# Moving one batch's attention from the hidden layer into the projection, and rearranging the conversion of float64 weights

## The chip, the cores and the metric

The kernel runs on one core of a Trainium2 chip. The metric is the device time of one execution in microseconds (us); the time of a kernel is the median of its runs.

## What is computed

The inputs are `x` (8 batches, 8 heads, 512 tokens, 64 features), `state` (8 batches, 8 heads, 32 states, 64 features), and the weights of a gated layer, which reach the kernel as float64. In the reference, cut to what matters:

```python
scores = scale * (x @ state.T);  a = softmax(scores);   xread = a @ state
scores2 = scale * (state @ x.T); a2 = softmax(scores2); sread = a2 @ x
y = concatenate([xread, sread], axis=2)          # (8, 8, 544, 64)
t = y.transpose(0, 2, 1, 3).reshape(8 * 544, 512)
tn = t / sqrt(mean(t * t) + 1e-6) * rms_g
out = (silu(tn @ w_gate) * (tn @ w_val)) @ w_out  # 512 -> 1536 -> 512
```

## The kernel before, in words

**Order of the work.** The program goes over the 8 batches. For each it computes attention, the hidden layer (1536 units in 12 blocks `m` of 128) and the projection to 512 columns; the states of all batches come at the end, as 256 rows together. `attention(b)` (L211) is a generator of 17 steps, and its steps are put between other work by `some(n)`, which takes the next n of them. Before the first hidden layer, attention of batch 0 runs alone up to its tokens, then values and the first four weight pieces, then the rest of attention of batch 0. In batch 0 the hidden layer is a loop over `m`; after every `m` it takes three steps of attention of batch 1, so that all 17 lie in the first six rounds. Batches 1 to 7 use another form, with seven products for eight blocks (`hidden_seven`, `project_seven`), and take steps of attention of the next batch in both. A scheduler lays the instructions of each engine out in a fixed order, by the order in the program and by when it reckons operands to be there; on the chip each engine then takes its instructions strictly in that order, and a waiting instruction holds those behind it.

**Weights.** A weight piece is 1 MB of float64: 128 partitions times 1024 pairs of 32-bit words. There are 18: twelve for gate and value (two for each pair of blocks `m`) and six for the output. `load_piece` (L134) loads up to four ahead, into four buffers, on SP's queue. `to_float32` (L163) turns a piece into float32, with eight operations: the exponent field is cut from the high words (L183, VectorE), clamped and moved into place by two Relu (L185, L186, ScalarE); the low words are scaled (L188, ScalarE Copy); the high mantissa gets its leading one (L189), is scaled and added to the low part (L190); the sign is put to the exponent (L192); and mantissa times exponent gives the weight (L196). L189 to L196 are VectorE's. `ready(n)` (L152) converts pieces up to n. Converted pieces of gate and value are also written back to a scratch in DRAM (L161), from which the later batches fetch them (L127); they share three buffers.

**Values and hidden layer.** `make_v` (L375) multiplies converted weights by the states (L381, PSUM pool `vps`) and copies the result out (L388). `hidden` (L401) multiplies it by the attention weights of the tokens (L407), and tanh (L412, ScalarE) and two VectorE operations (L413, L415) give the hidden block `hb`. In batch 0 the value product for a pair of blocks waits for two converted pieces.

**Projection of batch 0.** `project_as_ready` (L484) accumulates four PSUM banks over 12 blocks (L493), in the pools `fx`, `fy` and `fz`; before every second `m` it calls for one more converted piece of the output weights and then `between(m)`. At `m = 8` this converts all that is left, opens the buffers of the later batches in the space of the raw ones, and prepares batch 1: `slot_sums` (L428, four operations on GpSimd, POOL) and the first `make_v` of batch 1. Batch 1 begins with L445.

**Attention.** Transposes of x (L232) are copied out by ScalarE (L233); scores (L240, L249) are transposed (L259), reduced, shifted and exponentiated (L263 to L266), normalised (L273 to L276), transposed back (L281, L284) and multiplied by the states (L291). Only the mean of squares of this read is needed here: four Square on ScalarE (L297) give `sq`, two VectorE adds bring four blocks to one (L300, L301), four one-column matmuls sum over the partitions (L304), L307 adds the small constant, a power on POOL gives the inverse root (L206), which is spread by L209 and multiplied into the attention weights (L310). Then follow the states' reads (L316 to L347). At its start attention of batch b issues the loads of state and x of batch b + 1 (L83, L88). Its PSUM tiles come from `aps`, and two of the four reads from `vps`, which `make_v` uses too.

Of the kernel before, what the change touches and what calls it, by code (L numbers as in the profile page):

```python
# [8 lines left out]
F32 = mybir.dt.float32  # L9
I32 = mybir.dt.int32  # L10
U32 = mybir.dt.uint32
ALU = mybir.AluOpType
ACTF = mybir.ActivationFunctionType
AXX = mybir.AxisListType.X
# [2 lines left out]
P = 128  # L17
# [5 lines left out]
def kernel(  # L23
# [20 lines left out]
    VE, SE, GE, TE = nc.vector, nc.scalar, nc.gpsimd, nc.tensor  # L44
# [15 lines left out]
    two = ctx.enter_context(tc.tile_pool(name="two", bufs=2))  # L60
# [35 lines left out]
    ones = consts.tile([P, 1], F32, name="ones")  # L96
    GE.memset(ones, 1.0)
    bounds = consts.tile([P, 2], F32, name="bounds")
    GE.memset(bounds[:, 0:1], 1151.0)
    GE.memset(bounds[:, 1:2], 255.0 * (1 << 23))  # L100
    rms_g = consts.tile([P, NI], F32, name="rms_g")

# [26 lines left out]
    def home(k):  # L129
        if k >= NM:  # L130
            m = 2 * (k - NM)
            return wo[:, m:m + 2].rearrange("p m (i f) -> p m i f", f=P)
        mp = k // 2
        return (w_sb[mp] if k % 2 else new_w(mp))[:, :, :, k % 2, :]  # L134

    def load_piece(k):
        if k >= len(pieces):
            return
        src = pieces[k]
        if src.dtype == F32:  # L140
            return
        raw[k] = raws.tile([P, 8 * P, 2], I32, name="raw")
        out_ = raw[k].rearrange("p (a f) two -> p a (f two)", a=src.shape[1])
        for a in parts(k):
            nc.sync.dma_start(out=out_[:, a], in_=src[:, a].bitcast(I32))

    def parts(k):

        n = pieces[k].shape[1]
        return (slice(0, n // 2), slice(n // 2, n)) if k == 0 else (slice(0, n),)  # L150
# [13 lines left out]
    def to_float32(k):  # L164


        load_piece(k + RAW_AHEAD)
        to = home(k)
        if k not in raw:
            src = pieces[k].rearrange("p a (c f) -> p a c f", f=P)  # L170
            for a in range(src.shape[1]):
                nc.sync.dma_start(out=to[:, a], in_=src[:, a])
            return
        whole = raw.pop(k)
        tops = conv.tile([P, 8 * P], I32, name="top")
        exs = conv.tile([P, 8 * P], I32, name="ex")
        n = pieces[k].shape[1]
        for a in parts(k):
            cols = slice(8 * P * a.start // n, 8 * P * a.stop // n)
            r, top, ex, dst = whole[:, cols, :], tops[:, cols], exs[:, cols], to[:, a]  # L180
            hi = r[:, :, 1]
            man = r.bitcast(F32)[:, :, 0]
            VE.tensor_scalar(ex, hi, 20, 0x7ff, op0=ALU.logical_shift_right, op1=ALU.bitwise_and)  # L183

            SE.activation(out=ex, in_=ex, func=ACTF.Relu, scale=-1.0, bias=bounds[:, 0:1])  # L185
            SE.activation(out=ex, in_=ex, func=ACTF.Relu, scale=-float(1 << 23),  # L186
                          bias=bounds[:, 1:2])
            SE.activation(out=man, in_=r.bitcast(U32)[:, :, 0], func=ACTF.Copy, scale=2.0 ** -52)  # L188
            VE.tensor_scalar(top, hi, 0xfffff, 0x100000, op0=ALU.bitwise_and, op1=ALU.bitwise_or)  # L189
            VE.scalar_tensor_tensor(out=man, in0=top, scalar=2.0 ** -20, in1=man,  # L190
                                    op0=ALU.mult, op1=ALU.add)
            VE.scalar_tensor_tensor(out=ex, in0=hi, scalar=-(1 << 31), in1=ex,  # L192
                                    op0=ALU.bitwise_and, op1=ALU.bitwise_or)
            man, ex = (t.rearrange("p (a c f) -> p a c f", f=P, c=dst.shape[2])
                       for t in (man, ex.bitcast(F32)))
            VE.tensor_tensor(out=dst, in0=man, in1=ex, op=ALU.mult)  # L196


    stT_g = {}
# [3 lines left out]
    def inverse_rms(ss, n):  # L203

        ri = two.tile([P, NC], F32, name="ri")
        GE.tensor_tensor(out=ri[:, 0:n], in0=ss, in1=mhalf[:, 0:n], op=ALU.pow)  # L206
        rp = aps.tile([P, NC, P], F32, name="at")
# [4 lines left out]
    def attention(b):  # L212
        xb, packed = x_sb.pop(b), rows.pop(b)
        if b + 1 < B:
# [7 lines left out]
                     in_=packed.rearrange("p e d -> p (e d)"), identity=ident)  # L222
        VE.tensor_copy(stT, tp)
        VE.tensor_tensor(out=stT_g[b], in0=stT, in1=rms_g.unsqueeze(2).to_broadcast([P, 4, Ns]),
                         op=ALU.mult)
# [11 lines left out]
        sp = [aps.tile([P, S], F32, name="at") for e in range(2)]  # L237
        for j in range(4):
            for e in range(2):
                TE.matmul(out=sp[e][Ns * j:Ns * j + Ns, :], lhsT=stT[D * e:D * e + D, j, :],  # L240
                          rhs=xT[j // 2][D * e:D * e + D, j % 2].rearrange("p c t -> p (c t)"),
                          start=True, stop=True)
# [12 lines left out]
        for cp in range(2):  # L255
            tp = aps.tile([P, 2, 2, P], F32, name="at")
            for c in range(2):
                for e in range(2):
# [6 lines left out]
                             op=ALU.subtract)  # L265
# [4 lines left out]
        for cp in range(2):  # L270
# [6 lines left out]
                             op=ALU.mult)  # L277
            tp = aps.tile([P, 2, 2, P], F32, name="at")
            for c in range(2):
                for e in range(2):  # L280
                    TE.transpose(out=tp[:, c, e, :],  # L281
                                 in_=eS[:, 2 * cp + c, e].rearrange("p j n -> p (j n)"),
# [6 lines left out]
        for j in range(4):  # L289
            for e in range(2):  # L290
                TE.matmul(out=reads[j][D * e:D * e + D, :],  # L291
                          lhsT=packed[Ns * j:Ns * j + Ns, e, :],
                          rhs=aT[Ns * j:Ns * j + Ns, e].rearrange("n c t -> n (c t)"),
                          start=True, stop=True)
        sq = [one.tile([P, 2, S], F32, name="sq%d" % i, tag=("xT1", "eS")[i]) for i in range(2)]
        for j in (2, 3, 0, 1):
            SE.activation(out=sq[j // 2][:, j % 2, :], in_=reads[j], func=ACTF.Square,  # L297
                          scale=DM ** -0.5)
        yield
        VE.tensor_tensor(out=sq[1], in0=sq[1], in1=sq[0], op=ALU.add)  # L300
        VE.tensor_tensor(out=sq[0][:, 0, :], in0=sq[1][:, 0, :], in1=sq[1][:, 1, :], op=ALU.add)  # L301
        sp = aps.tile([P, NC], F32, name="at")
        for c in range(NC):
            TE.matmul(out=sp[:, c:c + 1], lhsT=sq[0][:, 0, P * c:P * c + P], rhs=ones,  # L304
                      start=True, stop=True)
        ss = two.tile([P, NC], F32, name="ss")
        VE.tensor_scalar(ss, sp, 1e-6, None, op0=ALU.add)  # L307
        yield
# [2 lines left out]
                         in1=rp.unsqueeze(1).to_broadcast([P, 2, S]), op=ALU.mult)  # L311
# [7 lines left out]
        for e in range(2):  # L319
            SE.activation(out=e2[:, e], in_=sS[:, e], func=ACTF.Exp, scale=SCALE,  # L320
                          bias=s2[:, e:e + 1], accum_out=z2[:, e:e + 1])
# [11 lines left out]
        for e in range(2):  # L333
            for c in range(NC):
                for j in range(4):
                    h = 2 * j + e
                    TE.matmul(out=rp[Ns * j:Ns * j + Ns, e, :],
                              lhsT=e2T[:, e, c, Ns * j:Ns * j + Ns],
                              rhs=xb[:, c, D * h:D * h + D],
                              start=(c == 0), stop=(c == NC - 1))  # L340
        sr = two.tile([P, 2 * D], F32, name="sr")
        for e in range(2):
            VE.tensor_scalar(sr[:, D * e:D * e + D], rp[:, e, :], z2[:, e:e + 1], None,
                             op0=ALU.mult)
# [5 lines left out]
    def state_norm():  # L350

        sq = one.tile([P, NI, NT], F32, name="sqT", tag="eS")
        SE.activation(out=sq, in_=xsT, func=ACTF.Square, scale=DM ** -0.5)
        sp = aps.tile([P, NT // P], F32, name="at")
        for r in range(NT // P):
            for i in range(NI):
                TE.matmul(out=sp[:, r:r + 1], lhsT=sq[:, i, P * r:P * r + P], rhs=ones,
                          start=(i == 0), stop=(i == NI - 1))
        ss = two.tile([P, NT // P], F32, name="sst")
        VE.tensor_scalar(ss, sp, 1e-6, None, op0=ALU.add)  # L360
        rp = inverse_rms(ss, NT // P)
        for i in range(NI):
            VE.scalar_tensor_tensor(out=xsT[:, i, :], in0=xsT[:, i, :], scalar=rms_g[:, i:i + 1],
                                    in1=rp[:, 0:NT], op0=ALU.mult, op1=ALU.mult)
        yield
# [257 lines left out]
    def some(n):  # L623
        for _ in range(n):
            next(steps, done)

    for b in range(B):
        if b > 0:
            steps = attention(b + 1) if b + 1 < B else state_norm()
        else:  # L630
            for m in range(NM):
                if m % 2 == 0 and m + 2 < NM:
                    make_v(b, m // 2 + 1)
                v, _ = v_sb[b, m // 2]
                hidden(m, S, lambda e, k: v[:, e, m % 2, k, :],
                       [aT_s[b][:, e, :] for e in range(2)])
                some(3)

            def between(m):
                if m == NM - 4:  # L640
                    ready(len(pieces))
                    early.close()
                    open_late()
                    prepare(b + 1)

            project_as_ready(store_tokens(b), between)
            sums = weight_sums()
        if b > 0:
            pairs = [hidden_seven(b, mp) for mp in range(NM // 2)]
            next(pairs[0])  # L650
            for mp, pair in enumerate(pairs):
                if mp + 1 < len(pairs):
                    make_v(b, mp + 1)
                next(pair)
                if mp + 1 < len(pairs):
                    next(pairs[mp + 1])
                next(pair)
                some(2)
                next(sums, done)
            project_seven(S, store_tokens(b), lambda: some(5), lambda: prepare(b + 1))  # L660
        for _ in steps:
            pass
        for _ in sums:
            pass
# [36 lines left out]
```

## Time and profile before

| what | value |
|---|---|
| median of three runs | 877.27 us (876.86 to 879.85) |
| the profiled execution's own time | 877.27 us |
| its span, first to last instruction | 875.5 us |
| PE (TensorE matmul) busy | 829.3 us, 95% |
| DVE (VectorE) busy | 473.2 us, 54% |
| ACT (ScalarE) busy | 341.6 us, 39% |
| POOL (GpSimd) busy | 156.2 us, 18% |
| TensorE's mean granted clock | 0.970 |
| first record of the hidden layer of batch 0 (L407) | 48.25 us |
| last conversion operation (L196) ends | 141.2 us |
| first record of batch 1's hidden layer (L445) | 161.68 us |

Times within the profile are counted from the first instruction. TensorE's matmuls overlap and their ends are modelled, so that a busy TensorE isn't one at its peak; a float32 matmul shows as two records, a transpose as one. Starts of successive records tell the pace better than the durations do. "Idle before, releaser" names what ended a wait. Shares over the whole span are means over stages with different limits, so the stages of the first 162 us have to be read by themselves.

### The profile page before, as it was taken

To read this page: it belongs to the slowest core of one execution; us is meant where nothing else is said; L and a number is where in the kernel's file an instruction comes from. 1 tells how busy PE (TensorE), PEld (TensorE's weight loads), DVE (VectorE), ACT (ScalarE), POOL (GpSimd) and SP (SyncE) were. 2 spreads that over 40 slices of the span, in tenths; PEclk is the share of its full clock that TensorE was granted. 3 is DMA by queue.
4 is the path that set the end of the run, shared out by engine and by line. 5 is a ranking of instruction groups with operands and counts; after the bars stand their busy time and mean duration, and the time that the engine had idled before them with its cause. 6 is when DMAs were issued, how large, how long until landed. Compare 5 with 4: busy or idle time off the path is not lost.

```text
span 875.5 us, 12043 instructions
## 1 busy us (share of the span) xinstructions
PE 829.3 (95%) x4806; PEld 607.8 (69%) x4806; DVE 473.2 (54%) x749; ACT 341.6 (39%) x571; POOL 156.2 (18%) x215
## 2 busy tenths in 40 slices
PE   3597999999999999999999999999999999999997
PEld 2152544577877778777877787777877787788886
DVE  5889898269216941486236922594158613651231
ACT  5678572364125520562136412652056313520110
POOL 0000005131122211330222112221132022300000
PEclk9598899999999999999999999999999999999999
DMA  9767771231242212330332123320242012301310
GB/s 283 252 206 248 246 267 49 103 137 52 50 144 98 97 45 91 131 123 4 89 141 108 52 61 133 107 86 1 85 155 99 1 64 92 141 41 37 109 48 25
DMA packets 61592, 94.11 MB, mean 107 GB/s; under 512 B 38752, under 2 KB 46432, under 8 KB 54624
## 3 DMA queue, kind: packets, MB, share of 16 engines
q1 hardware_dynamic: 57376, 92.29, 31.5%
q10 hardware_dynamic: 4160, 1.05, 0.5%
q8 instruction: 38, 0.62, 0.3%
q14 instruction: 18, 0.15, 0.0%
HBM read 78.12 MB, written 15.20 MB: 107 GB/s over the span
## 4 chain that ended last, share of the span: by engine, by line
PE 78%; DVE 11%; ACT 7%; DMA 2%; issue 1%; SPq 1%; POOL 0%; ACTq 0%; DVEq 0%
PE f L536 29%; PE f L445 24%; PE f L407 7%; PE pv L381 5%; PE f L493 5%; ACT sq L297 2%; PE at L240 1%; ACT e L320 1%; PE at L232 1%; PE at L304 1%; DMA raw<-in_moe_w_val_dram 1%; DVE m L316 1%; PE at L291 1%; DVE hb L475 1%; DVE hb L471 1%
## 5 line engine op out<-in xcount | busy, mean ns | idle before, releaser
L445 PE MATMUL f<-aT_s,v 128*128 128x256 f32 x504 | 131.9, 394 | 2.8 <-ACT g L462 2.8
L536 PE MATMUL f<-wo,hb 128*128 128x256 f32 x540 | 127.7, 394 | 0.0
L445 PEld LDWEIGHTS f<-aT_s,v 128*128 128x128 f32 x504 | 89.4, 189 | 52.9 <-issue 29.8
L536 PEld LDWEIGHTS f<-wo,hb 128*128 128x128 f32 x540 | 106.2, 199 | 17.3 <-ACT ot L556 1.9
L388 ACT COPY v<-pv 128x512 f32<-128x512 f32 x96 | 51.7, 591 | 112.3 <-PE pv L381 112.2
L556 ACT COPY ot<-f 128x256 f32<-128x256 f32 x60 | 19.6, 375 | 194.0 <-PE f L536 184.8
L396 POOL TENSOR_TENSOR vs<-v 128x256 f32<-128x256 f32 x42 | 30.6, 728 | 323.3 <-ACT v L388 323.3
L536 PE MATMUL f<-wt,hs 128*128 128x256 f32 x360 | 87.9, 390 | 0.0
L445 PE MATMUL f<-aT_t,vs 128*128 128x256 f32 x336 | 86.3, 379 | 0.0
L460 DVE TENSOR_TENSOR g<-g,f 128x512 f32<-128x512 f32 x42 | 28.7, 683 | 89.4 <-PE f L445 62.9
L536 PEld LDWEIGHTS f<-wt,hs 128*128 128x128 f32 x360 | 64.7, 190 | 16.3 <-issue 4.9
L561 DVE TENSOR_TENSOR ot<-ot,f 128x256 f32<-128x256 f32 x45 | 17.0, 417 | 104.5 <-issue 53.2
L381 PE MATMUL pv<-w_m,stT_g 64*32 64x512 f32 x768 | 67.1, 628 | 6.8 <-ACT sq L297 6.1
L445 PEld LDWEIGHTS f<-aT_t,vs 128*128 128x128 f32 x336 | 63.8, 190 | 9.5 <-issue 0.8
L470 ACT ACTIVATE hb<-g 128x1024 f32<-128x1024 f32 x42 | 44.4, 1057 | 34.5 <-DVE g L464 34.5
L471 DVE SCALAR_TENSOR_TENSOR hb<-hb,g 128x1024 f32<-128x1024 f32 x42 | 51.5, 1225 | 7.3 <-ACT hb L470 7.3
L407 PE MATMUL f<-aT_s,v 128*128 128x512 f32 x96 | 46.8, 627 | 2.3 <-ACT v L388 2.3
L206 POOL TENSOR_TENSOR ri<-ss,mhalf 128x4 f32<-128x4 f32 x8 | 9.4, 1179 | 191.2 <-DVE ss L307 150.0
L445 PE MATMUL f<-aT_t,v 128*128 128x256 f32 x168 | 43.1, 379 | 0.0
L445 PE MATMUL f<-aT_s,vs 128*128 128x256 f32 x168 | 43.1, 379 | 0.0
L493 PE MATMUL f<-wo,hb 128*128 128x512 f32 x96 | 41.6, 593 | 0.0
L407 PE MATMUL f<-xsT,w_m 128*128 128x256 f32 x192 | 41.6, 379 | 0.0
(114 smaller groups left out, 1253.3 us busy)
## 6 DMA issues: line engine op xcount, KB each, us to landing
w_m<-w_d SPq DMA_DIRECT2D x48, 1024.0 KB, 4.8
x_b<-in_x_dram SPq DMA_DIRECT2D x28, 256.0 KB, 4.0
out_dram<-ot SPq DMA_DIRECT2D x56, 128.0 KB, 1.8
raw<-in_moe_w_val_dram SPq DMA_DIRECT2D x6, 1024.0 KB, 6.5
w_d<-w_m SPq DMA_DIRECT2D x6, 1024.0 KB, 8.6
raw<-in_moe_w_out_dram SPq DMA_DIRECT2D x6, 1024.0 KB, 6.8
raw<-in_moe_w_gate_dram SPq DMA_DIRECT2D x5, 1024.0 KB, 7.1
x_b<-in_x_dram ACTq DMA_DIRECT2D x4, 256.0 KB, 5.1
```

The source lines that it names most:

```text
L297: SE.activation(out=sq[j // 2][:, j % 2, :], in_=reads[j], func=ACTF.Square, scale=DM ** -0.5)
L381: TE.matmul(out=pv[e][Ns * j:Ns * j + Ns, :], lhsT=stT_g[b][D * e:D * e + D, j, :], rhs=w[D * e:D * e + D, j].rearrange("p m k f -> p (m k ...
L388: SE.copy(v[:, e].rearrange("p m k f -> p (m k f)"), pv[e])
L396: GE.tensor_tensor(out=vs[:, 0], in0=a21, in1=a22, op=ALU.add)
L407: TE.matmul(out=ps[:, 0:n], lhsT=lhs(i, k), rhs=r, start=(i == 0), stop=(i == len(rhs) - 1))
L445: TE.matmul(out=ps[:, i, :], lhsT=lhs[:, i, :], rhs=rhs, start=(start and i == 0), stop=True, skip_group_check=True)
L460: VE.tensor_tensor(out=g[:, :, 0, :], in0=g[:, :, 0, :], in1=ys, op=ALU.add)
L470: SE.activation(out=h, in_=gate, func=ACTF.Tanh, scale=0.5)
L471: VE.scalar_tensor_tensor(out=h, in0=h, scalar=1.0, in1=gate, op0=ALU.add, op1=ALU.mult)
L493: TE.matmul(out=op, lhsT=hb[:, m, P * r:P * r + P], rhs=wo[:, m, :], start=(m == 0), stop=(m == NM - 1))
L536: TE.matmul(out=ps[:, r, :], lhsT=lhs(k)[:, P * r:P * r + P], rhs=rhs(k), start=(start and r == 0 and k == 0), stop=(k == HM - 1), skip_gr ...
L556: SE.copy(kept[r], ps[:, r, :])
```

## The change

Three things change. In the conversion, the exponent is no longer cut out by VectorE: ScalarE takes the absolute value of the high word (read as a float), then the first Relu reads the upper 16 bits of the result as an integer, scales by 1/16 and rounds it to the exponent with a suitable constant. The low words are no longer scaled by ScalarE: VectorE's addition takes them as integers, and the power of two comes in with the last operation. In attention of batch 0 alone, the four blocks of squares are summed by 16 accumulating one-column matmuls in place of two adds and four matmuls. And the steps of attention of batch 1 move from the hidden layer (three after each `m`) into the projection (five before every second `m`).

```diff
-    GE.memset(bounds[:, 0:1], 1151.0)
+    GE.memset(bounds[:, 0:1], 1151.0 + 7.5 / 16)
...
             hi = r[:, :, 1]
+            lo = r.bitcast(U32)[:, :, 0]
             man = r.bitcast(F32)[:, :, 0]
-            VE.tensor_scalar(ex, hi, 20, 0x7ff, op0=ALU.logical_shift_right, op1=ALU.bitwise_and)
-
-            SE.activation(out=ex, in_=ex, func=ACTF.Relu, scale=-1.0, bias=bounds[:, 0:1])
+            SE.activation(out=ex.bitcast(F32), in_=r.bitcast(F32)[:, :, 1], func=ACTF.Abs)
+            SE.activation(out=ex, in_=ex.bitcast(U16).rearrange("p (f two) -> p f two", two=2)[:, :, 1],
+                          func=ACTF.Relu, scale=-1.0 / 16, bias=bounds[:, 0:1])
             SE.activation(out=ex, in_=ex, func=ACTF.Relu, scale=-float(1 << 23),
                           bias=bounds[:, 1:2])
-            SE.activation(out=man, in_=r.bitcast(U32)[:, :, 0], func=ACTF.Copy, scale=2.0 ** -52)
             VE.tensor_scalar(top, hi, 0xfffff, 0x100000, op0=ALU.bitwise_and, op1=ALU.bitwise_or)
-            VE.scalar_tensor_tensor(out=man, in0=top, scalar=2.0 ** -20, in1=man,
+            VE.scalar_tensor_tensor(out=man, in0=top, scalar=2.0 ** 32, in1=lo,
                                     op0=ALU.mult, op1=ALU.add)
             VE.scalar_tensor_tensor(out=ex, in0=hi, scalar=-(1 << 31), in1=ex,
                                     op0=ALU.bitwise_and, op1=ALU.bitwise_or)
...
-            VE.tensor_tensor(out=dst, in0=man, in1=ex, op=ALU.mult)
+            VE.scalar_tensor_tensor(out=dst, in0=man, scalar=2.0 ** -52, in1=ex,
+                                    op0=ALU.mult, op1=ALU.mult)
...
-        VE.tensor_tensor(out=sq[1], in0=sq[1], in1=sq[0], op=ALU.add)
-        VE.tensor_tensor(out=sq[0][:, 0, :], in0=sq[1][:, 0, :], in1=sq[1][:, 1, :], op=ALU.add)
+        parts_ = [sq[j // 2][:, j % 2, :] for j in (2, 3, 0, 1)]
+        if b > 0:
+            VE.tensor_tensor(out=sq[1], in0=sq[1], in1=sq[0], op=ALU.add)
+            VE.tensor_tensor(out=parts_[2], in0=sq[1][:, 0, :], in1=sq[1][:, 1, :], op=ALU.add)
+            parts_ = [parts_[2]]
         sp = aps.tile([P, NC], F32, name="at")
         for c in range(NC):
-            TE.matmul(out=sp[:, c:c + 1], lhsT=sq[0][:, 0, P * c:P * c + P], rhs=ones,
-                      start=True, stop=True)
+            for i, part in enumerate(parts_):
+                TE.matmul(out=sp[:, c:c + 1], lhsT=part[:, P * c:P * c + P], rhs=ones,
+                          start=(i == 0), stop=(i == len(parts_) - 1))
...
                 hidden(m, S, lambda e, k: v[:, e, m % 2, k, :],
                        [aT_s[b][:, e, :] for e in range(2)])
-                some(3)
 
             def between(m):
+                some(5)
                 if m == NM - 4:
                     ready(len(pieces))
                     early.close()
```

More of the change, by code (lines that the diff above doesn't have):

```diff
@@ L11 @@
 U32 = mybir.dt.uint32
+U16 = mybir.dt.uint16
 ALU = mybir.AluOpType
```

## The prediction

> **What bounds the kernel now.** I read the page's first part, then a table of stages, then the chain of waits, then the timeline around the places where the chain leaves TensorE. The table of stages has the start, then the hidden layer of batch 0 (from its first matmul), its projection, and batch 1:
>
> ```profile
> core 0: us, PE busy (x) PEld busy (x) DVE busy (x) ACT busy (x) POOL busy (x), PEclk, DMA share, GB/s
> 0.00:48.20 48.20, 25.01 (x117) 10.97 (x118) 32.51 (x53) 28.25 (x41) 2.24 (x11) 0.72 0.84 266
> 48.20:112.30 64.10, 56.78 (x371) 26.38 (x369) 59.27 (x89) 46.18 (x66) 1.92 (x1) 0.92 0.74 235
> 112.30:161.70 49.40, 49.40 (x129) 21.50 (x130) 37.72 (x46) 20.46 (x23) 12.20 (x8) 1.00 0.36 128
> 161.70:255.00 93.30, 91.45 (x574) 70.08 (x573) 47.57 (x76) 35.12 (x62) 20.80 (x29) 1.00 0.29 97
> ```
>
> The columns are busy microseconds with counts. In the second row VectorE (DVE) is busy 59.27 of 64.10 us, and TensorE (PE) is not full. In the third PE is full and VectorE has 11.7 us free. From batch 1 on nothing that the change touches runs, so only the time at which batch 1 starts (161.7) can move. The chain says the same in order of time:
>
> ```profile
> 70.97 0.59 DVE t L413
> 71.56 0.09 DVE z L274
> 71.65 0.59 DVE z L273
> 72.24 0.16 DVE z L275
> ...
> 112.29 7.13 PE f L407 x16
> 119.43 27.47 PE f L493 x64
> ```
>
> The first numbers are start and length. Up to 79 us the chain hops along VectorE, through attention of batch 1, the weights' conversion and the hidden layer's own two operations; from 112.3 it is TensorE alone. Between the two, attention costs TensorE waits and its clock:
>
> ```profile
> 81.93 1.07 ACT L297 ACTIVATE sq<-pv 128x512 f32<-128x512 f32 x2
> 82.57 2.44 PE L381 MATMUL pv<-w_m,stT_g 64*32 64x512 f32 x16 [3.39 <-ACT sq L297]
> 85.73 2.07 PE L407 MATMUL f<-aT_s,v 128*128 128x512 f32 x2 [0.71 <-ACT v L388]
> ```
>
> The bracket is the idle time before it: 3.39 us for banks that the squares hold. Two records of L407 then take 2.07 us against 0.86 at full clock.
>
> **What the Trainium skill says.** "TensorE: Matmul & The Clock Gate", Part 1: about 3.4 us of an idle array halve its clock, and as much sustained work restores it. The trace agrees: the granted clock is 0.50 from 84 to 92 us. The same page, section LDWEIGHTS: the load costs by the columns of the weights, not by the result's width; here eight one-column records of L304 take 1.87 us at half clock (40.31), 1.02 us at full clock (219.10). "VectorE: DVE Perf Modes", perf-mode tier table: fp32 with one tensor source runs at twice the rate of two. The trace agrees: L183 and L189 take 687 ns, L190, L192 and L196 take 1211 to 1226 ns. "ScalarE: Activation LUTs", Table sets: abs and relu are in every set; so no further table load is expected. Before has one, of 1283 ns; no run yet shows Abs.
>
> **Part 1, the conversion.** VectorE does five operations on each of 18 pieces. They start 0.60 us apart for L183 and L189 and 1.14 apart for the other three: 2 x 0.60 + 3 x 1.14 = 4.6 us. L183 goes; L190 reads an integer tensor in place of a float one, and L196 becomes a two-source operation of the same kind as L190: both kept at 1.14. So 4.0 us a piece, 18 x 0.60 = 10.8 us in all, 8 x 0.60 = 4.8 of it on the pieces 4 to 11 that the hidden layer waits for. ScalarE keeps three operations a piece of 1.15 us (Abs for Copy): nothing, and it was busy 46.2 of 64.1 us. The strided 16-bit input of the new Relu is shown by no row: taken at 1.15 us like L185; at twice that, 8 x 1.15 = 9 us more on ScalarE would still fit into its 18 free us.
>
> **Part 2, squares of batch 0.** Away go L300 and L301 on VectorE (1.14 + 0.60 = 1.7 us). 16 one-column matmuls in place of 4 are 32 records for 8. At half clock that is 32 x 0.23 = 7.5 us, 5.6 more; at full clock 32 x 0.13 = 4.1, 2.2 more. Before, the last square ended at 35.74 and L304 at 42.18, 6.4 us later, since the adds waited in VectorE's queue and TensorE was busy with values. After, 7.5 us at half clock, and the squares end some 2 us sooner, as four pieces have given back 2.4 us by then. Behind L304 wait the POOL power, L209 and L310 as now. I take 1.5 us gained: hidden layer from 46.7 instead of 48.2 (bounds: 44.5 if TensorE warms up during this row of matmuls; 49.5 if value matmuls go between them).
>
> **Part 3, attention of batch 1 moves.** Out of the hidden layer go, on VectorE, its reductions, subtractions, products and copies: twelve of 0.60 and three of 1.14 and small ones, 10.9 us; on ScalarE some 10 us; on TensorE, at full clock by the rows of the same lines in batches 0 and 1: L232 2.1, L240 1.06, L259 1.04, L281 0.9, L291 1.0, L304 1.0, L209 0.45, L327 0.9, L337 1.3, others 0.25: 10.0 us.
>
> *The hidden layer.* VectorE, from L307 (42.2) to the end of piece 11 (108.8), 66.6 us: 8 pieces 36.8, attention of batch 1 10.9, rest of batch 0's 2.3, 17 hidden operations 10.3, so 6.3 idle. After: 32.0 + 2.3 + 10.3 + 4 idle = 48.6, and 1 us ahead at the start (conversion of piece 4 before L307; bounds 0 and 4): piece 11 at about 90. What is late next is TensorE: from 46.7, 2 us of batch 0's states, ten m of 3.57 us (16 records of L407 take 7.13) and four value products of 1.08 bring it to 88.7: both come to the same point. Then value product and copy (2.7 us as a chain), and m = 10 and 11 (7.1): the projection starts at 99.5, against 119.3.
>
> *The projection.* 96 records of L493: 27.63 us for 64 and 14.00 for 32, 41.6; one value product 1.1; now also attention 10.0, all on the path, since TensorE is full here. Between two of the six calls of five steps lie 16 records, 6.9 us; 17 steps take the first four gaps. VectorE has six pieces x 4.0 + 10.9 = 35 of 52 us, ScalarE 6 x 3.3 + 10 + 2.3 = 32. A new wait: a matmul of attention whose operand is late holds the records of L493 queued behind it, and nobody else. In batch 1, where attention lies among the projection's matmuls likewise, L304 waits 1.29 us and L536 0.8 us: 2 us. With the conversion in VectorE's queue I take 3 (bounds 1 and 10). End: 99.5 + 41.6 + 1.1 + 10.0 + 3 = 155.2.
>
> *Other queues.* SP: attention of batch 1 also issues the load of batch 2's x (four of 256 KB) and state (four of 16 KB); they move behind the raw loads, and batch 2's x is first used at 179: nothing; without that cover one landing, 4 to 7 us. POOL: its power (1.9 us) must precede the slot sums of batch 1 (9.5 us from the last conversion, 141.3 to 150.8). Conversion ends near 137, sums near 147, before 155: nothing; if it ended after 143, each us would be one.
>
> **The sum.** Batch 1 starts at 155.2 instead of 161.7: 6.5 us less. The profiled execution took 877.27 us, 1.77 more than its span; it is also the median of the three runs. 877.3 - 6.5 = 870.8.
>
> **The rivals.** *More gain.* TensorE is warm early (hidden layer from 44.5) and never waits for weights: 44.5 + 2 + 12 x 3.57 + 4 x 1.08 + 2 = 95.7, projection with 1 us of waits to 149.4: 12.3 us less, 865.0. For it: VectorE would no longer be full. Against: a pair of pieces and two m cost VectorE 8.0 + 2.4 = 10.4 us, TensorE 8.2. *Weights' transfers take over.* Each pair brings 2 MB, writes 1 MB back, and fetches up to 1 MB for batch 1: 4 MB at the 315 GB/s that full stretches reach (266 / 0.84) is 12.7 us against 10.4; three pairs: 7 us, projection from 106, end 161.7 less what four buffers ahead hide (1 us): 876.3. For it: a DMA share of 0.74 already. Against: raw pieces wait in their buffers (piece 11 was issued at 76.0, converted from 99.7), and batch 2's x leaves this stage. *Slower: TensorE waits in the projection.* Some ten times attention goes from TensorE to VectorE or ScalarE and back. If each time its operand sits behind one conversion operation more (1.14 us and the 0.3 of a handover) and TensorE stands, that is 14 us, and 2 more at half clock: 99.5 + 52.7 + 16 = 168.2, 6.5 us more, 883.8. It turns to a loss at 9.5 us of waits. For it: the hidden layer lost about 11 us so (113.4 us for 102 of work). Against: VectorE was 92% busy there, and is 67% busy here.
>
> **How the numbers follow.** A measurement of this kernel tells about 0.5% (4.4 us: 872.9 to 881.7) from no change. Forecast 870.8, chance 0.50, own range 867.5 to 874.5, four fifths of it below 872.9; more gain 0.15; transfers or the like, no change, 0.19; waits, slower, 0.16. Faster 0.40 + 0.15 = 0.55; same 0.10 + 0.19 = 0.29; slower 0.16. The range goes from 864.0 to 878.0: the forecast, most of the two gains and the transfer case; left out are the loss and the far ends.
>
> **What would show it.** Right: no L183; 17 or 18 groups of Abs near 1.15 us; L304 of batch 0 with 32 records of about 7 us; first L407 near 46.7; first L493 near 99.5, half clock gone between 84 and 92; attention's lines between 100 and 137 with few us of waits; first L445 near 155. Wrong: VectorE still full with long waits for raw tiles (transfers), TensorE idle between records of L493, or slot sums on POOL ending after L493.

## The result, and the profile after

The changed kernel takes 883.57 us (median of four runs, 883.07 to 885.37) against 878.56 us for the kernel before, measured beside it: a ratio of 1.0061, with a 95% interval of 1.0033 to 1.0089. It is slower by 0.6%, where 0.7% less was forecast. The profiled execution took 883.85 us with a span of 882.0 us.

In the changed kernel the lines have other numbers: L188, L189 and L191 are Abs and the two Relu; L194, L196 and L200 are the former L190, L192 and L196; L313 are the column matmuls over the squares (L304 before), L316 the constant after them (L307), L390 the value products (L381), L336 and L346 the states' part of attention (L327, L337), L416 the hidden layer (L407), L502 the projection (L493), L454 batch 1 (L445); L302 is the Square (L297), L211 and L214 the power and its spreading (L206, L209), L397 the copy of the value products (L388). In the experiments' kernels the same lines lie a few numbers off; there the names say which is meant: `pv` the value products, `sq` and `ones` the column matmuls, `f` the hidden layer. The table of stages of the changed kernel, over the same stretches as before:

```profile
core 0: us, PE busy (x) PEld busy (x) DVE busy (x) ACT busy (x) POOL busy (x), PEclk, DMA share, GB/s
0.00:48.20 48.20, 24.92 (x114) 14.45 (x117) 27.13 (x42) 26.63 (x37) 2.70 (x11) 0.74 0.82 264
48.20:112.30 64.10, 60.84 (x261) 24.63 (x256) 53.13 (x68) 45.78 (x56) 0.00 (x0) 0.85 0.67 239
112.30:161.70 49.40, 47.23 (x240) 21.94 (x239) 36.81 (x55) 22.05 (x32) 8.17 (x9) 0.97 0.40 119
```

VectorE is indeed relieved: 117.1 us of work up to 161.7 instead of 129.5, 12.4 us, where the conversion (10.8) and the adds (1.7) were to give 12.5. But in the second row it is busy only 53.1 of 64.1 us, and the granted clock is lower than before (0.85 against 0.92). The stages themselves, from first records:

| kernel | first hidden matmul | first projection matmul | batch 1 starts |
|---|---|---|---|
| before | 48.3 | 119.3 | 161.7 |
| forecast | 46.7 | 99.5 | 155.2 |
| changed | 58.9 | 114.7 | 169.2 |

The hidden layer takes 55.8 us (forecast 52.8, before 71.0) and the projection 54.5 (forecast 55.7, before 42.4). The projection did what was forecast, the hidden layer took 3.0 us more. The greater part of the loss lies ahead of them: the hidden layer starts 12.2 us later than forecast. The chain of waits of the changed kernel shows that stretch (start, length, engine, line, records):

```profile
35.15 0.59 PE at L313 x2
35.74 1.86 PE pv L390 x8
37.60 6.50 PE at L313 x30
...
44.44 1.87 POOL ri L211
46.36 1.12 PE at L214 x4
47.47 1.86 PE pv L390 x6
49.33 1.04 PE at L336 x4
50.37 1.84 PE pv L390 x2
52.22 1.04 PE at L336 x4
53.26 1.01 PE at L346 x32
54.27 1.84 PE pv L390 x2
56.12 1.01 PE at L346 x32
57.13 1.88 PE pv L390 x12
59.00 2.00 PE f L416 x2
```

From the first column matmul to the first hidden matmul almost everything is TensorE. Two things are to be seen. The column matmuls take 7.1 us. And the value products, 32 records, take 11.1 us in six portions (the sixth, two records at 44.0, lies beside the wait for POOL): a portion of two records takes as long (1.84) as one of eight (1.86) or twelve (1.88). The records of one value product lie in different rows and columns of the array and run at the same time; where other matmuls stand between them, each portion pays the full length.

The granted clock over the same stretch of the changed kernel (columns: TensorE busy, records, clock, DMA share, GB/s):

```profile
36.00:40.00 4.00, 4.00 (x20) 0.50 1.02 366
40.00:44.00 4.00, 4.00 (x20) 0.50 0.98 395
44.00:48.00 4.00, 3.57 (x10) 0.50 0.03 14
48.00:52.00 4.00, 4.00 (x12) 0.50 0.00 0
52.00:56.00 4.00, 4.00 (x39) 0.50 0.00 0
56.00:60.00 4.00, 4.00 (x47) 0.50 0.01 4
60.00:64.00 4.00, 4.00 (x11) 0.89 0.81 261
```

TensorE counts as busy nearly all the time, and still it has half its clock until about 61 us; in the kernel before it was at full by 48:

```profile
44.00:48.00 4.00, 4.00 (x23) 0.54 0.65 253
```

From 44 us the transfers stop too: no raw load is issued between 35.6 and 58.9, since the conversion of the next pieces stands in ScalarE's and VectorE's queues behind operations that wait for TensorE (L316 7.4 us, L397 9.7 us): L194, whose operands were there at 36.8, starts at 44.2, right behind L316. So the row of column matmuls delays the weights too. Without the squares part (run e1_cm below) the last operation on the next piece starts at 46.9 us and those on the last two pieces at 87.0; here they start at 57.6 and 98.9. From 62 us on the chain of the changed kernel runs mostly through these conversions and the hidden layer's own operations, on ScalarE and VectorE.

### The profile page after: what moved, and what is told of

It reads as the page before. It is cut to its first block, busy times and chain, and to the rows that moved or that the text cites. A ratio compares the mean times of both kernels' runs of the same rounds, so it can differ in the third digit from the quotient of the medians.

```text
span 882.0 us, 12089 instructions
## 1 busy us (share of the span) xinstructions
PE 837.9 (95%) x4830; PEld 613.2 (70%) x4830; DVE 461.5 (52%) x728; ACT 343.4 (39%) x571; POOL 150.6 (17%) x215
## 4 chain that ended last, share of the span: by engine, by line
PE 74%; DVE 13%; ACT 8%; DMA 2%; issue 2%; SPq 0%; POOL 0%; ACTq 0%; DVEq 0%; POOLq 0%
PE f L545 29%; PE f L454 24%; PE f L416 5%; PE pv L390 5%; PE f L502 3%; PE at L313 2%; PE at L237 2%; ACT sq L302 1%; PE at L245 1%; ACT ex L188 1%; DVE m L325 1%; ACT e L329 1%; DVE ex L196 1%; PE at L336 1%; DVE sq L307 1%
## 5 line engine op out<-in xcount | busy, mean ns | idle before, releaser
L454 PE MATMUL f<-aT_s,v 128*128 128x256 f32 x504 | 131.9, 394 | 2.8 <-ACT g L471 2.8
L454 PEld LDWEIGHTS f<-aT_s,v 128*128 128x128 f32 x504 | 89.4, 189 | 52.9 <-issue 29.8
L397 ACT COPY v<-pv 128x512 f32<-128x512 f32 x96 | 51.7, 591 | 118.9 <-PE pv L390 118.9
L454 PE MATMUL f<-aT_t,vs 128*128 128x256 f32 x336 | 86.3, 379 | 0.0
L390 PE MATMUL pv<-w_m,stT_g 64*32 64x512 f32 x768 | 68.5, 624 | 2.8 <-DVE w_m L200 2.8
L454 PEld LDWEIGHTS f<-aT_t,vs 128*128 128x128 f32 x336 | 63.8, 190 | 9.5 <-issue 0.8
L480 DVE SCALAR_TENSOR_TENSOR hb<-hb,g 128x1024 f32<-128x1024 f32 x42 | 51.5, 1225 | 7.2 <-ACT hb L479 7.2
L211 POOL TENSOR_TENSOR ri<-ss,mhalf 128x4 f32<-128x4 f32 x8 | 9.4, 1170 | 244.2 <-DVE ss L316 244.2
L416 PE MATMUL f<-aT_s,v 128*128 128x512 f32 x96 | 45.4, 628 | 0.4 <-ACT v L397 0.4
L502 PE MATMUL f<-wo,hb 128*128 128x512 f32 x96 | 44.5, 608 | 0.0
L454 PE MATMUL f<-aT_t,v 128*128 128x256 f32 x168 | 43.1, 379 | 0.0
L454 PE MATMUL f<-aT_s,vs 128*128 128x256 f32 x168 | 43.1, 379 | 0.0
L416 PE MATMUL f<-xsT,w_m 128*128 128x256 f32 x192 | 41.6, 379 | 0.0
```

What stands on the lines that cost most here:

```text
L390: TE.matmul(out=pv[e][Ns * j:Ns * j + Ns, :], lhsT=stT_g[b][D * e:D * e + D, j, :], rhs=w[D * e:D * e + D, j].rearrange("p m k f -> p (m k ...
L397: SE.copy(v[:, e].rearrange("p m k f -> p (m k f)"), pv[e])
L416: TE.matmul(out=ps[:, 0:n], lhsT=lhs(i, k), rhs=r, start=(i == 0), stop=(i == len(rhs) - 1))
L454: TE.matmul(out=ps[:, i, :], lhsT=lhs[:, i, :], rhs=rhs, start=(start and i == 0), stop=True, skip_group_check=True)
L480: VE.scalar_tensor_tensor(out=h, in0=h, scalar=1.0, in1=gate, op0=ALU.add, op1=ALU.mult)
L502: TE.matmul(out=op, lhsT=hb[:, m, P * r:P * r + P], rhs=wo[:, m, :], start=(m == 0), stop=(m == NM - 1))
```

## The experiments

**The parts one by one.** Theory A blames the squares of batch 0, B the move of attention, C the conversion through ScalarE. Conversion and move without the squares:

```diff
-        parts_ = [sq[j // 2][:, j % 2, :] for j in (2, 3, 0, 1)]
...
+        VE.tensor_tensor(out=sq[1], in0=sq[1], in1=sq[0], op=ALU.add)
+        VE.tensor_tensor(out=sq[0][:, 0, :], in0=sq[1][:, 0, :], in1=sq[1][:, 1, :], op=ALU.add)
```

> The changed kernel with the two VectorE adds and four column matmuls put back for batch 0 (squares undone; conversion and move kept). Theory A (the 32 records of column matmuls at half clock, and the value products that they push behind themselves, delay the hidden layer): first hidden matmul near 47 instead of 58.9 us, batch 1 near 157, total near 872. Theory B (moving attention costs it, through another order or waits in the projection): first hidden matmul stays near 58, total near 883. Theory C (the conversion's chain through ScalarE holds VectorE up): total near 880 or more, with long waits of L196 for L191.

Measured: 875.27 us, ratio to before 0.9964 (0.9952 to 0.9976). First hidden matmul at 49.3, projection from 100.8, batch 1 at 157.9. The squares part alone, put into the kernel before (the diff of the change for those lines, and nothing else):

> The kernel before with only the squares of batch 0 on TensorE. Theory A: the first hidden matmul comes some 8 to 10 us later than at 48.2, total near 886. Theories B and C: squares alone cost or gain under 2 us, total 877 to 880.

Measured: 885.62 us, ratio 1.0075 (1.0055 to 1.0094); first hidden matmul at 55.7, batch 1 at 171.9. The move of attention alone:

```diff
-                some(3)
 
             def between(m):
+                some(5)
```

> The kernel before with only the steps of attention of batch 1 moved into the projection. Theory A: hidden layer from near 48, shorter by attention's 10.9 us of VectorE, projection longer by 10 of TensorE and 2 to 3 of waits: total 876 to 881. Theory B: total 884 or more, the loss being in the projection or in a later start of the hidden layer. Theory C says nothing here.

Measured: 881.68 us, ratio 1.0039 (1.0026 to 1.0053), just above A's range; hidden layer from 47.9 to the projection at 109.4, batch 1 at 165.4. The hidden layer is 9.4 us shorter than before and the projection 13.5 longer. And the conversion alone (the diff of the change for its lines):

> The kernel before with only the new conversion. Theory A: VectorE has 0.6 us less per piece, 12 pieces before the projection: 6 to 7 us less, total near 871. Theory C: no gain or a loss, total 878 or more, VectorE waiting for the last Relu on ScalarE. Theory B says nothing here.

Measured: 879.19 us, ratio 1.0006 (0.9990 to 1.0021); first hidden matmul at 49.9, batch 1 at 164.2. So the squares cost 7.6 us in the one kernel (885.62 against 878.01) and 8.3 in the other (883.57 against 875.27): A holds, and the squares account for more than the whole loss. B and C are out as the cause of it. But A's number for the conversion alone, 871, was missed clearly: alone it gives nothing, and the move alone costs 0.4%; only the two together gain. Table of stages, conversion alone, then conversion and move together:

```profile
48.20:112.30 64.10, 60.67 (x357) 27.04 (x356) 52.92 (x78) 45.62 (x63) 1.39 (x1) 0.84 0.67 226
```

```profile
48.20:112.30 64.10, 61.31 (x280) 25.68 (x280) 60.09 (x74) 50.44 (x61) 0.00 (x0) 0.98 0.86 290
```

With the conversion alone VectorE has 6.4 us less to do than before in this stretch and stands for as many more; the clock is 0.84. The chain of that kernel shows why:

```profile
83.68 4.57 PE pv L386 x24
88.24 2.00 PE f L412 x2
90.25 1.84 PE pv L386 x2
92.09 1.80 PE at L309 x8
93.89 1.85 PE pv L386 x6
```

Attention of batch 1 still holds TensorE: from 83.7 to 97.7 us value products, column matmuls and hidden matmuls run at a clock of 0.50 (L412 2.00 us for two records against 0.86). The hidden layer is about as long as before (71.9 us against 71.0), with TensorE busy for 68.5 of it. Once attention is out of it, the weights' conversion is its bound (with the move alone VectorE is busy for 58.5 of 61.6 us, and the chain stays on it from 57 to 98), and then the cheaper conversion pays: 61.5 us with the move alone, 51.5 with both. With both, VectorE is no longer alone in the chain: it carries it from 57 to 72 us, and from there to the projection it lies mostly on ScalarE's part of the conversion and one write-back of a converted piece (10.64 us from 76.4).

**What in the squares part costs?** It takes two adds from VectorE, gives TensorE 24 more records, and thereby changes TensorE's order: most value products come behind the column matmuls. Theory A1 blames the records, A2 the order. First the program of the changed kernel with the column matmuls cut to 8 (only one block of squares is summed for batch 0: three quarters of the mean of squares are left out, so the output is not the layer's):

```diff
-        parts_ = [sq[j // 2][:, j % 2, :] for j in (2, 3, 0, 1)]
+        parts_ = [sq[j // 2][:, j % 2, :] for j in ((2, 3, 0, 1) if b > 0 else (2,))]
```

> The changed kernel whose column matmuls for batch 0 take only one of the four blocks of squares (8 records; three quarters of the mean of squares are left out there), with no adds. TensorE's order keeps most value products behind them, as in the changed kernel. Theory A1 (the 24 further records at half clock, 0.215 us each, are the loss): first hidden matmul near 49, total near 875. Theory A2 (the order is the loss: value products that lie behind the column matmuls and run at half clock ahead of the hidden layer): first hidden matmul 54 or later, total 879 or more.

Measured: 871.61 us, ratio 0.9928 (0.9909 to 0.9946); first hidden matmul at 44.1, batch 1 at 154.8. Better than A1 expected: with 8 records it also waits for one square only, and its clock is up from 41 us; and its value products come in four portions, not six, so that A2 is tested only in part. Next the reverse, the adds kept and the same block summed four times:

```diff
+            n_ = 4 if b == 0 else 1
+            for i in range(n_):
+                TE.matmul(out=sp[:, c:c + 1], lhsT=sq[0][:, 0, P * c:P * c + P],
+                          rhs=quarter if b == 0 else ones, start=(i == 0), stop=(i == n_ - 1))
...
```

> The changed kernel with the adds put back for batch 0 and the one block's column matmuls done four times with ones of 0.25 (32 records; same result); TensorE's order is that of the kernel without the squares part, value products first. Theory A1: 24 records more at 0.215 us on the path, first hidden matmul near 54.5, total near 880.5. Theory A2: the first hidden matmul within 2 us of 49.3, total near 876; anything between gives the share of each.

Measured: 880.37 us, ratio 1.0026 (1.0013 to 1.0039), 5.1 us more than without the 24 records; first hidden matmul at 52.6, batch 1 at 164.5. The total is A1's, the start is 1.9 us better than its 54.5, because here the clock was up when the column matmuls began (they took 3.99 us). The timeline of this kernel, then its clock:

```profile
35.52 6.08 PE L390 MATMUL pv<-w_m,stT_g 64*32 64x512 f32 x32 [1.63 <-ACT sq L304]
41.53 3.99 PE L313 MATMUL at<-quarter,sq 128*128 128x1 f32 x32
47.85 1.12 PE L216 MATMUL at<-ident,ri 128*128 128x128 f32 x4 [2.33 <-POOL ri L213]
```

```profile
36.00:40.00 4.00, 4.00 (x25) 0.50 1.02 366
40.00:44.00 4.00, 4.00 (x37) 0.82 1.04 421
44.00:48.00 4.00, 1.67 (x13) 0.61 0.09 31
48.00:52.00 4.00, 3.32 (x32) 0.50 0.00 0
```

The value products, all 32 records with no other matmul between them, take 6.1 us, and at their end the clock is up; by the end of the row of column matmuls it is at half again, until beyond 52 us. A dose between, one add kept and two blocks summed (16 records):

```diff
+        VE.tensor_tensor(out=sq[1], in0=sq[1], in1=sq[0], op=ALU.add)
+        parts_ = [sq[1][:, 0, :], sq[1][:, 1, :], sq[0][:, 0, :]]
+        if b == 0:
+            parts_ = parts_[:2]
...
```

> The changed kernel with one of the two adds kept for batch 0 and two blocks summed by the column matmuls (16 records). Theory A1: 8 x 0.215 = 1.7 us more than with both adds, less 0.7 for the add saved: first hidden near 50.5, total near 876.5. Theory A2: half of the value products lie behind, a loss of 3 to 5 us, total near 879.

Measured: 876.27 us, ratio 0.9981 (0.9970 to 0.9992), first hidden matmul at 50.2: A1's number. And the whole change with the first two value products ahead in the program:

```diff
+    for _ in range(11):
+        next(steps)
+    make_v(0, 0)
+    make_v(0, 1)
     while next(steps) != "tokens":
         pass
-    make_v(0, 0)
-    ready(4)
...
-                if m % 2 == 0 and m + 2 < NM:
+                if m % 2 == 0 and 0 < m and m + 2 < NM:
```

> The whole change, but with the first two value products put into the program ahead of the column matmuls of batch 0, so that TensorE does them while the squares are made (32 records, no adds). Theory A1: the records still cost, first hidden matmul 53 to 55, total near 880. Theory A2: first hidden matmul near 50, total near 876.

Measured: 879.91 us, ratio 1.0022 (1.0011 to 1.0032), first hidden matmul at 55.6. The records are the larger share (A1: 880; 4.6 us of time above the kernel without the squares), and the order is real too: 3.3 us of start and 3.7 us of time against the changed kernel, with the value products now in three portions and 5.9 us instead of six and 11.1.

**Is it the clock?** Theory A3 says yes. Eight matmuls of no use fill TensorE's idle time in attention of batch 0, so that its clock is up before the column matmuls:

```diff
+        busy = fx.tile([P, S], F32, name="f") if b == 0 else None
+        def work(n, rhs):
+            for _ in range(n if b == 0 else 0):
+                TE.matmul(out=busy, lhsT=ident, rhs=rhs, start=True, stop=True)
...
```

> The whole change, with eight further 512-column matmuls of no use put on TensorE during attention of batch 0, where it has no other work, so that its clock has been asked for before the column matmuls. Theory A3 (the half clock makes the loss: all that lies between the squares and the hidden layer runs at half pace, and column matmuls don't raise the clock): column matmuls near 0.12 us a record, first hidden matmul 50 to 52 instead of 58.9, total near 876. Theory A1 alone (only the number of records counts): the clock changes nothing of it, first hidden matmul 57 or later, total 882 or more.

Measured: 876.88 us, ratio 0.9991 (0.9974 to 1.0009), first hidden matmul at 51.4. Its timeline and clock:

```profile
37.49 4.14 PE L322 MATMUL at<-ones,sq 128*128 128x1 f32 x32 [0.78 <-ACT sq L311]
41.56 1.91 PE L399 MATMUL pv<-w_m,stT_g 64*32 64x512 f32 x2
...
44.95 1.95 PE L399 MATMUL pv<-w_m,stT_g 64*32 64x512 f32 x14
...
48.41 1.05 PE L399 MATMUL pv<-w_m,stT_g 64*32 64x512 f32 x4
...
50.42 1.08 PE L399 MATMUL pv<-w_m,stT_g 64*32 64x512 f32 x12
```

```profile
36.00:40.00 4.00, 3.12 (x22) 1.00 1.02 418
40.00:44.00 4.00, 3.57 (x17) 0.65 1.02 348
44.00:48.00 4.00, 4.00 (x24) 0.50 0.75 310
48.00:52.00 4.00, 4.00 (x86) 1.00 0.23 43
```

The same 32 records take 4.14 us instead of 7.1. The time is 6.7 us below the changed kernel's and 1.6 above that without the squares. Not all of this is the clock, since TensorE's order is better too: the value products come in four portions, not six. From the first column matmul to the first hidden matmul TensorE takes 13.9 us here and 23.8 in the changed kernel. Of these 9.9 us the two portions fewer are worth some 3.7 (an estimate: 2 x 1.85), and the clock the other 6; the first column matmul itself comes 2.3 us later, behind the useless matmuls. So by this estimate the half clock carries the larger part of the loss; no run varies the clock with the order held. The same matmuls without the squares part:

> Conversion and move without the squares part, with eight such matmuls of no use. Theory A3: what lies between squares and hidden layer, some 11 us of TensorE at half clock, takes 6: first hidden matmul near 45 to 46 instead of 49.3, total near 871. Theory A1: no change, 49 and 875.

Measured: 877.65 us, ratio 0.9991 (0.9978 to 1.0005), first hidden matmul at 50.0. A3's 871 was missed: the useless matmuls pushed attention back (value products begin at 37.1 instead of 35.4), and before 44 us the clock had fallen again.

**Can the combination be bettered?** Four steps instead of five per gap of the projection:

> Conversion and move without the squares part, with four instead of five steps of attention before every second m of the projection. If the projection's waits (1.8 us for the squares and 1.7 of half clock after it) come from steps lying too close: 2 us less, total near 873. If they come from VectorE's queue: no change, 875.

Measured: 878.72 us, ratio 0.9996 (0.9983 to 1.0009): rather worse than five (0.9964), where the expectation had a gain or no change. No usable trace of it exists, so why stays open. And the states' reads of batch 0 within the hidden layer:

```diff
-    for _ in states_read:
-        pass
...
                        [aT_s[b][:, e, :] for e in range(2)])
+                next(states_read, done)
```

> Conversion and move without the squares part, with the rest of batch 0's attention (its states' reads) taken up within the hidden layer, one step after each m, instead of ahead of it. If TensorE at half clock between the squares and the hidden layer sets the start, the hidden layer starts 2 to 3 us sooner (near 47 instead of 49.3) and total is near 873; if the hidden layer's length is set by the weights' conversion alone, its end doesn't move, and total stays at 875.

Measured: 876.37 us, ratio 0.9974 (0.9962 to 0.9986). The hidden layer starts at 47.7, 1.6 us sooner, and the projection at 101.1 instead of 100.8: the end of the hidden layer is set by the conversion, as the second half of the expectation says (the last two pieces come at 87.4, against 87.0). Conversion and move without the squares (875.27) stays the best of the versions that do the whole computation; it is 0.4% faster than the kernel before.

## Why the prediction was wrong

**The step that failed is Part 2**: "I take 1.5 us gained: hidden layer from 46.7 instead of 48.2 (bounds: 44.5 ...; 49.5 if value matmuls go between them)". It came at 58.9. Without the squares it is 49.3, so this part moved it by 9.6 us later instead of 1.5 sooner. (The 1.5 is more than the part's own terms give: squares ending at 35.7 - 2 and 7.5 us of column matmuls end at 41.2, against 42.2 before, a gain of 0.9.) Compare TensorE from the first record after the squares to the first hidden matmul, changed kernel against the one without squares. This is the latter's timeline:

```profile
35.36 5.89 PE L386 MATMUL pv<-w_m,stT_g 64*32 64x512 f32 x32 [1.63 <-ACT sq L302]
41.18 1.05 PE L309 MATMUL at<-ones,sq 128*128 128x1 f32 x8
44.56 1.11 PE L214 MATMUL at<-ident,ri 128*128 128x128 f32 x4 [2.33 <-POOL ri L211]
45.47 1.06 PE L332 MATMUL at<-ident,e 128*128 128x128 f32 x4
47.21 1.12 PE L332 MATMUL at<-ident,e 128*128 128x128 f32 x4 [0.68 <-ACT e2T L333]
48.25 1.08 PE L342 MATMUL at<-x_b,e2T 128*32 128x64 f32 x32
49.26 2.04 PE L412 MATMUL f<-aT_s,v 128*128 128x512 f32 x2
```

Column matmuls: 1.0 us here, 7.1 there, +6.1. Value products: 5.8 and 11.1, +5.3. The other matmuls: 4.0 and 5.2, +1.2, one half of L346 being among them that otherwise comes later. Waits of TensorE: 3.0 and 0.4, -2.6. The sum is 10.0; 23.8 us (35.15 to 58.93) less 13.9 (35.36 to 49.26) is 9.9. Besides this row, the conversion came later too, as shown above, and the hidden layer was longer: 55.8 us instead of 51.5. Three assumptions were wrong:

1. The price of the records was right (7.5 us estimated, 7.1 measured), but their place was not free. I set them against the 6.4 us in which VectorE's adds and TensorE's wait had stood. In that time TensorE did value products, which the first hidden matmul needs as well. Moving the adds to TensorE put both in a row on the engine that sets this start.
2. "If value matmuls go between them" was priced at some 3 us (49.5 - 46.7). Broken into six portions they cost 5.3 us by themselves.
3. The end of the squares didn't come 2 us sooner. It was at 36.6 (35.7 before): the last Square waits in ScalarE's queue behind Abs and Relu of the next pieces. And the clock came up near 61 us, not before 48: the 7.5 us assumed half clock for the records alone, but all that followed them ran at half pace as well, and with the clock up beforehand and two portions fewer (e9) the time was 6.7 us less.

**Part 1** was right in its prices: Abs has a median of 1.152 us and the 16-bit Relu 1.149 us, the sole table load stays (1.283 us, now at 3.7 us, ahead of the data), which agrees with what was cited of "ScalarE: Activation LUTs", Table sets; VectorE's work fell as reckoned. Wrong was its "nothing" for ScalarE: it looked at ScalarE's free time in the hidden layer, not at its queue ahead of it. With the new conversion and the adds kept, the copies and Squares of batch 0 stand behind Abs and Relu, the last Square ends at 36.8 instead of 35.7, and the hidden layer starts at 49.3 (49.9 without the move) instead of 48.2. **Part 3** was right too: without the squares the hidden layer took 51.5 us (52.8 forecast), the projection 57.1 (55.7), with TensorE waiting 1.8 us for the adds of batch 1. Both parts alone would have forecast 161.7 - 156.7 = 5.0 us; 2.7 were measured. In the two profiled executions batch 1 starts 3.8 us sooner, and from there to the end it takes 714.6 us instead of 713.8, which the sum held to be fixed. I left unsaid that part 1 gains nothing unless part 3 takes attention away: the two were in one sum.

**The rivals.** The slower one gave 883.8 us, close to the time measured, and for the wrong reason: it wanted 68.7 us of projection with 16 us of waits, and the projection took 54.5, with one wait of 2.17 us for the adds of batch 1. *Transfers* did not become the bound of the changed kernel: its hidden layer ran at a DMA share of 0.81, and VectorE's longest wait there for a raw tile was 1.07 us. The 315 GB/s of this rival were too low besides: 366 to 421 GB/s were reached above at a share near 1. *More gain* fell with Part 2.

## What to carry to other kernels

Before work is moved to an engine because another one is full elsewhere, list what the engine does in that very stretch and add the new work to it, and look at what stands behind it in the other engines' queues; a wait in its row is not free time if work that the next stage needs fills it. Matmuls that run side by side in parts of the array should stay together in the order: one instruction between them costs a whole length. And a saving on one engine counts only once what else binds the same stage is gone, so parts that lean on each other should be forecast, and tried, as pairs.

## What was not expected of the hardware

A row of one-column matmuls with full weight loads does not keep TensorE's clock up, though the trace shows TensorE busy. In the changed kernel 6.5 us of them (37.6 to 44.1) ran at half clock to the end, and the clock stayed at 0.50 until about 61 us, though other matmuls followed; what held it down there no run separates. In e6 and e9 the clock was full when the row began and fell within it: a mean of 0.61 over 44 to 48 us puts the fall at 44.9, 3.4 us after the row's start at 41.5 and ahead of its end at 45.5; 0.65 over 40 to 44 puts it at 41.2, 3.7 us after 37.5 and ahead of 41.6. That fits the 3.4 us of an idle array that "TensorE: Matmul & The Clock Gate", Part 1, of the Trainium skill states, if such a row counts as idle; the page doesn't say that, and of what makes it so no run here shows more. At half clock a record of the row cost 0.215 us, at full clock 0.125 to 0.13. Two records of a value product took 1.84 us alone, and so did eight together (1.86).
